# Input sums of two residues copied into PSUM ahead of the decay products, with the hand-written order of steps changed

## The chip, the cores and the metric

The kernel runs on one core of one Trainium2 chip. The time is the device time of one execution in microseconds; of several runs the median is given. A core has TensorE (PE, matrix products into PSUM), VectorE (DVE), ScalarE (ACT), GpSimd (POOL) and SyncE (SP, which here only issues DMAs). PSUM has eight banks, and a tile of 128 partitions by 512 f32 values fills one of them.

## The reference

For x of 2048 positions by 512 channels, two branches are mixed by a gate per position. Branch A is a diagonal complex state-space model with 512 states, branch B a linear attention with 32 heads of 16 and a softmax feature map. Cut to what matters here:

```python
# branch A: h_t = Lam_bar * h_{t-1} + (B_bar x_t),  y = 2 Re(C h) + D x
Bu = jnp.einsum("bld,pd->blp", x + 0j, B_bar)
for t in range(L):
    h = Lam_bar[None, :] * h + Bu[:, t, :]
# branch B: phi = concat(softmax(p), softmax(-p));  kv = sum phi_k v;  o = phi_q kv / phi_q z
o = num / den
# mix
out = g * a + (1 - g) * (o @ wo)
```

## The kernel before

Everything stays on the chip between the loads of the inputs and the stores of the output. The kernel is written as some 200 small generators, called steps (`st_...`), each of which issues a few instructions up to its next `yield`. The string `ORDER` is a list of 855 names. The loop at line 804 takes one name after the other and runs that generator one piece on. The four engines PE, DVE, ACT and SP execute their instructions in exactly this order, so the list is the schedule, written out by hand. Behind a name, `@5` gives the PSUM bank (or banks) that the piece takes, `:D` sends its copy or scaling to VectorE instead of ScalarE, `:A` an output's DMA to ScalarE's queue, and `F:28` puts 28 small idle matmuls (`spin`) on TensorE. The digit is the step's index; a name that comes twice runs its two pieces.

**Branch A.** The positions are dealt into eight residues r (position modulo 8), each with 256 positions. The states make four groups j of 128 states, each as two halves h of 64 states with real and imaginary parts.

- `l8` to `l15` load tiles of x transposed (tiles 0 to 7 are loaded ahead of the list). `NR` and `NI` load the two parts of B (`Bn`), `R0` to `R7` transpose it, `C..` and `J..` load C, `Q..` the query weights, `O` the output weights. All go through SyncE's queue. `c0` to `c7` scale C, two products and a sum each. `i0` to `i3` make the tables of sines and cosines.
- `g` r j (line 597) sums eight matmuls of x with B and, for odd r, products of the decay with the neighbours before. The result is the input sum that a block of positions up to r brings in. For r below 7 it is evicted to SBUF as `uv[j][:, r]` in bf16, for r = 7 to `va`.
- `z` j (line 622) runs the recurrence over the 256 blocks on VectorE and leaves the state at residue 7 in `H7`.
- `h` r j (line 660) makes the states of residue r: a power of the decay, as a diagonal block `dg`, times a state already there, plus `uv`. There are two ways to add `uv`. For the 20 pairs of `H_VECTOR` (r in 1, 2, 4, 5, 6) VectorE adds it while it evicts (line 672). For the other eight (r in 0, 3) TensorE multiplies `uv` by the identity (line 667) ahead of the decay's product (line 668), two matmuls of each per step, and ScalarE evicts (line 674). Residues 0, 1, 3 and 5 and their successors start from `H7`, so all `h` steps come behind their `z`.
- `y` n (line 711) multiplies the states of an output tile by C: two halves of four 512-column matmuls, and a tail of four 128-column ones with x and D. It accumulates in a PSUM bank that stays taken until `t` n.

**Branch B.** `W` and `f` fold the feature map into the key weights, `w` into the query weights. `k`, `v`, `q` n project tile n (four 512-column matmuls and an eviction). The features of keys (groups 0 to 4) and queries (groups A and 1 to 3) go through `x`/`X` (maximum tree and subtraction), `n`/`N` (the same with the minimum), `e`/`E` (exponentials on ScalarE, four tiles) and `s`/`S` (sums and normalisation on VectorE, with two small functions on ScalarE between). For queries `S` ends with four DMA transposes into `phT` (line 563). `a` n accumulates keys times values in two PSUM banks, which are given back by `Y` and `G` (the gate). `END` closes the first half's buffers; the query groups 1 to 3 come behind it.

`o` n (line 725) is the attention's numerator and denominator of tile n: two groups `pn` of four small matmuls from `phT`, evictions, a product on VectorE (`on`), and a transpose to `oT`, by DMA for n below 12 and on TensorE from 12 on. Tiles 0 to 3 use the features of group A, 4 to 7 those of group 1, 8 to 11 of group 2, 12 to 15 of group 3. `t` n (line 761) adds the output projection to y's bank, scales by the gate into `ot` and stores.

Of the kernel before, what the change touches and what calls it, by code (L numbers as in the profile page):

```python
# [29 lines left out]
k14 a0 n2 s1 k12 g20 x2 g00@6 k9 g30@0 s1 s1 s1 x2 n2 s1 v3 g40@4 x3 g01@3 g10@7 n3 R5 g00 a1 a1 x3 g60@1 n3 e2 R4  # L30
g11@6 g10 x3 g01 n3 e2 x3 e2 e2 n3 g11 k15@3 g60 g10 g30 g40 x3 s2 n3 g70@1 k15 g11 s2 x4 s2 s2 n4 g30 Q1 Q3 x4 n4 e3
e3 x4 C5 n4 Q0 x4 g50@7 g50 g50 s2 g21@4 n4 g21 s2 s2 v8@3 e3 e3 s3 g70 g70 g70 z0 s3 z0 g31@6 g31 s3 z0 z0 v11@0
g41@7 a2 C6 a2 g41 z0 z0 v11 g61@4 a2 g61 C7 w0@1 w0 C3 w1@7 w1 g31 a2 w2@0 w2 w3@4 s3 s3 g51@1 g51 g51 z0 R7 z0 x4
g62@7 w3 z0 z0 g71@6 g71 g02@0 v8 n4 s3 J2 g71 g71 z1 g02 z1 h50@1 h50 J2 z1 e4 e4 q1@4 h10@3 g62 g12@6 h10 g22@0 q2@1
z1 z1 z1 g22 q2 s3 z1 z1 q1 e4 h60@3 h60 g12 g12 z1 q3@7 q0@0 q0 q3 g32@1 e4 xA C2 g42@4 g32 nA g32 s4 g42 v9@6 v9 z1
s4 C0 J0 J0 g52@0 g52 c4 g52 nA c4 xA c4 R6 g72@7 g72 J1 s4 nA g23@3 g43@1 g03@4 g63@6 g72 g72 z2 h51@0 J3 c5 a3 g23
z2 J1 v10@7 h11@3 nA a3 c2 c2 g03 xA z2 z2 z2 z2 c0 h51 h61@4 z2 z2 g13@0 v10 xA h11 g43 c3 g13 a3 a3 J3 c5 z2 s4
g33@7 g13 g33 c0 z2 s4 s4 g33 h32@1 c2 h32 xA g53@3 g63 h52@0 g53 g53 nA s4 h52 h42@7 h42 eA c5 eA v14@1 v14 g73@6 g73
g73 q5@3 g73 h61 h12@0 h12 v12@1 v15@7 z3 z3 c0 z3 v12 eA eA h21@4 z3 v13@6 h21 a4 z3 z3 sA v13 z3 z3 c3 q10@0 q10
# [5 lines left out]
o2 y1 o2 t1 S1 S1 G G y9@5 y9 E2 E2 y4@2 y4 y2 N3 E2 E2 y5@6 y9 y5 t1 S1 S1 S1 S1 X3 t3 t3 y2 t2 t2 X3 N3 N3 S2 X3 S2
t0 o4@7 y5 o4 o4@4 o4 N3 o4 X3 S2 y4 t0 y13@0 S2 o4 o5@7 o5 o5@4 o5 o5 y6 o4 y6 o6@3 S2 o6 o6@7 o6 X3 o5 y7@4 y7 o5 S2
S2 o7@3 N3 y13 o6 t4 t0:A o6 o6 E3 E3 E3 S2 S2 y8@7 t4:D o7:D E3 S3 t5 S2 S2 S2 t5 y12@2 S3 S3 o7@3 o7 o7 o7 t6 t6
o8@6 o8 o8@3 o8 o7 y12 y8 S3 t1:A o8 o8 o9@1 o9 o9@6 o8 y11@3 y11 S3 S3 y10@1 o9 o9 o9 S3 S3 t4:A o11@6 y7 t7 y12 o9
o11 t7 o10@6 y8 t8 t8 y11 y13 o11@4 t9 S3 S3 S3 o10 o11 S3 o10@7 t9:D y15@6 y14@4 o11 o11 o10 o10 t8:A o12@7 o12 o12@5
# [19 lines left out]
def kernel(  # L69
# [44 lines left out]
    def bank(shape, dtype, name):  # L114
        return ps.tile(shape, dtype, tag=f"t{sel['banks'].pop(0)}", name=name, bufs=1)

    def evac(out_ap, in_ap):
        if sel["eng"] == "act":
            nc.scalar.copy(out=out_ap, in_=in_ap)  # L119
        else:  # L120
            nc.vector.tensor_copy(out=out_ap, in_=in_ap)
# [57 lines left out]
    G = const.tile([P, NTI], F32, name="G")  # L179
# [479 lines left out]

    def st_h(r, j):  # L660
        ph = bank([P, 2, NC], F32, "ph")
        add = (r, j) in H_VECTOR
        for h in range(2):
            t = 2 * j + h
            src = hs(r - 1, t, slice(0, NC)) if r in (2, 4, 6) else hs(7, t, slice(-1, NC - 1))
            if not add:
                MM(out=ph[:, h, :], lhsT=ident[:], rhs=uv[j][:, r, h, :], start=(h == 0), stop=False, skip_group_check=True)
            MM(out=ph[:, h, :], lhsT=dg[:, (r + 1) // 2 if r % 2 else 0, t, :], rhs=src, start=(add and h == 0), stop=True, skip_group_check=True)
# [179 lines left out]
```

## Time and profile before

| | us |
|---|---|
| median of 3 runs | 156.07 |
| lowest and highest | 155.94, 157.04 |
| the profiled execution, its own time | 156.63 |
| its span, first to last instruction | 154.6 |
| TensorE's weight loads, busy | 95.6 |
| GpSimd busy, all before 25 us | 16.1 |

The span leaves out about 2 us at the two ends. Busy time of an engine counts an instruction from its start to its end, and neighbours overlap by a part of their time. So the distance from one start to the next, which the timeline gives, is the better price of an instruction in a row of equal ones. TensorE's granted clock is 1.0 throughout.

This is how the busy shares go along the span, in 40 slices of 3.9 us:

```
PE   7999999999999999999999999999998999989990
DVE  3789999999999999999999999999997966423730
ACT  3489999999999999999999996799497998465652
DMA  4785998465475849910000006943169689789742
```

### The profile page before, as it was taken

Reading aid. Unit: us, or ns where it says so; the run is one execution under the profiler, and the core shown is the slowest. Engines: PE = TensorE matmul, PEld = TensorE weight load, DVE = VectorE, ACT = ScalarE, POOL = GpSimd, SP = SyncE. Lnnn points to the kernel's source line nnn. Section 1 sums busy time; section 2 is a strip of 40 time slices with the busy share of each in tenths; the row PEclk is TensorE's granted clock in tenths of the full one; section 3 lists DMA queues with packets and bytes.
Section 4 is the critical chain, followed back from the end, with each engine's and each line's share of the span. In section 5 each row is a group of like instructions: output and inputs, shape, how many; then the busy total and the mean of one; then the engine's idle time right before and its main releaser. Section 6 shows DMA issues by size and latency. Waiting matters only on the chain.

```text
span 154.6 us, 3382 instructions
## 1 busy us (share of the span) xinstructions
PE 147.7 (96%) x1254; PEld 95.6 (62%) x1254; DVE 131.8 (85%) x303; ACT 129.4 (84%) x279; POOL 16.1 (10%) x43
## 2 busy tenths in 40 slices
PE   7999999999999999999999999999998999989990
PEld 7844444797789876888755767454454545545540
DVE  3789999999999999999999999999997966423730
ACT  3489999999999999999999996799497998465652
POOL 8239980000000000000000000000000000000000
PEclk9999999999999999999999999999999999999999
DMA  4785998465475849910000006943169689789742
GB/s 120 158 222 87 168 191 170 89 98 107 97 78 105 174 94 168 184 25 6 0 0 4 0 0 136 141 136 68 34 123 143 117 163 197 150 137 200 208 147 94
DMA packets 50848, 17.55 MB, mean 113 GB/s; under 512 B 44176, under 2 KB 50832, under 8 KB 50832
## 3 DMA queue, kind: packets, MB, share of 16 engines
q1 hardware_dynamic: 48544, 15.36, 53.2%
q10 hardware_dynamic: 2128, 1.97, 4.5%
q8 instruction: 10, 0.16, 0.4%
q14 instruction: 6, 0.05, 0.1%
q0 software_dynamic: 160, 0.01, 0.1%
HBM read 2.64 MB, written 2.10 MB: 31 GB/s over the span
## 4 chain that ended last, share of the span: by engine, by line
DVE 47%; PE 32%; DMA 8%; ACT 6%; issue 4%; DVEq 0%; SPq 0%
PE py L717 9%; DVE smk L511 6%; PE pk L475 6%; DMA oT<-on 5%; PE py L765 5%; PE pgq L601 4%; DMA phT<-EEq 3%; DVE Bn L672 3%; DVE EEk L548 3%; DVE w L641 3%; DVE HM L672 3%; DVE H L652 3%; PE spin L812 3%; DVE EEk L527 2%; DVE EEk L521 2%
## 5 line engine op out<-in xcount | busy, mean ns | idle before, releaser
L601 PE MATMUL pgq<-xT,BT 128*128 128x256 bf16 x256 | 31.2, 272 | 0.0
L475 PEld LDWEIGHTS <-xT 128*128 128x128 bf16 x192 | 18.3, 98 | 18.6 <-DMA xT<-in_A_x_dram 0.8
L601 PEld LDWEIGHTS <-BT 128*128 128x128 bf16 x256 | 24.7, 98 | 3.9
L138 ACT ACTIVATE EEk<-EEk 128x1024 bf16<-128x1024 bf16 x20 | 20.6, 1075 | 0.3 <-DVE EEk L527 0.3
L765 PE MATMUL py<-Wo,oT 128*128 128x512 bf16 x64 | 16.1, 379 | 0.9 <-DMA oT<-on 0.9
L119 ACT CAST uv<-pgq 128x512 bf16<-128x512 f32 x28 | 16.3, 604 | 0.3
L475 PE MATMUL pq<-Wq,xT 128*128 128x512 bf16 x64 | 15.8, 379 | 0.0
L475 PE MATMUL pv<-Wv,xT 128*128 128x512 bf16 x64 | 15.6, 379 | 0.0
L475 PE MATMUL pk<-Wk,xT 128*128 128x512 bf16 x64 | 15.0, 379 | 0.3 <-ACT EEk L138 0.3
L138 ACT ACTIVATE ld<-pn 128x16 f32<-128x16 f32 x32 | 6.2, 193 | 7.6 <-PE pn L736 7.4
L138 ACT ACTIVATE EEq<-EEq 128x1024 bf16<-128x1024 bf16 x12 | 11.8, 1061 | 0.3 <-DVE EEq L527 0.3
L590 ACT ACTIVATE phT<-X,dgB 128x512 bf16<-128x512 bf16 x16 | 11.5, 740 | 0.0
L769 ACT ACTIVATE ot<-py,G 128x512 bf16<-128x512 f32 x12 | 8.0, 684 | 3.5 <-PE py L765 3.3
L119 ACT CAST nu<-pn 128x256 bf16<-128x256 f32 x28 | 10.3, 381 | 0.0
L736 PEld LDWEIGHTS <-phT 128*128 128x128 bf16 x128 | 6.7, 98 | 5.3 <-DMA phT<-EEq 1.2
L765 PEld LDWEIGHTS <-oT 128*128 128x128 bf16 x64 | 5.6, 97 | 6.2 <-DMA oT<-on 1.2
L119 ACT CAST vx<-pv 128x512 bf16<-128x512 f32 x16 | 9.4, 600 | 0.0
L548 DVE TENSOR_TENSOR EEk<-EEk,rck 128x4096 bf16<-128x4096 bf16 (+1 forms) x5 | 9.3, 1859 | 0.0
L119 ACT CAST Xq<-pq 128x512 bf16<-128x512 f32 x16 | 9.1, 610 | 0.2
L736 PE MATMUL pn<-KVm,phT 128*128 128x68 bf16 x128 | 8.0, 194 | 0.8 <-DMA phT<-EEq 0.7
L119 ACT CAST Xq<-pk 128x512 bf16<-128x512 f32 x15 | 8.4, 618 | 0.4 <-PE pk L475 0.4
L511 DVE TENSOR_TENSOR smk<-smk 128x512 bf16<-128x512 bf16 (+4 forms) x18 | 8.6, 476 | 0.1
(177 smaller groups left out, 319.6 us busy)
## 6 DMA issues: line engine op xcount, KB each, us to landing
X<-HM SPq DMA_DIRECT2D x8, 256.0 KB, 4.0
out_dram<-ot ACTq DMA_DIRECT2D x11, 128.0 KB, 2.5
out_dram<-ot SPq DMA_DIRECT2D x5, 128.0 KB, 2.5
C2r<-in_B_wqkv_dram ACTq DMA_DIRECT2D x2, 256.0 KB, 3.3
Wv<-in_B_wqkv_dram SPq DMA_DIRECT2D x1, 512.0 KB, 4.0
Bn<-in_A_B_re_dram SPq DMA_DIRECT2D x1, 512.0 KB, 5.5
Bn<-in_A_B_im_dram SPq DMA_DIRECT2D x1, 512.0 KB, 6.7
Wo<-in_B_wo_dram SPq DMA_DIRECT2D x1, 512.0 KB, 4.6
```

The lines of the kernel that those rows point to most:

```text
L119: nc.scalar.copy(out=out_ap, in_=in_ap)
L138: ins = nc.scalar.activation(**kw)
L475: MM(out=pt[:], lhsT=xT[:, kt, ti * P:(ti + 1) * P], rhs=W[:, kt, :], start=(kt == 0), stop=(kt == KT - 1))
L511: VT(out=dst, in0=cur[:, :, :, 0:n, :], in1=cur[:, :, :, n:2 * n, :], op=op)
L548: VT(out=E5, in0=E5, in1=rc.to_broadcast([P, L, 2 * NB, Dh, 4]), op=ALU.mult)
L590: nc.scalar.mul(out=t_, in_=x_, mul=c_)
L601: MM(out=pg[:, h, :], lhsT=BT[:, kt, 2 * j + h, :], rhs=xT[:, kt, r * NC:(r + 1) * NC], start=(h == 0 and kt == 0), stop=(r % 2 == 0 and k ...
L672: VT(out=dst, in0=ph[:], in1=uv[j][:, r], op=ALU.add)
L717: MM(out=py[:], lhsT=hs(r, t, slice(a * P, (a + 1) * P)), rhs=C2B[t], start=(t == 0), stop=False)
L736: MM(out=pn[:, 4 * m:4 * m + 4, :].rearrange("p h e -> p (h e)"), lhsT=ph[:, 4 * hf + m, :], rhs=KVm[:, 4 * hf + m, :], start=(m == 0), st ...
L765: MM(out=py[:], lhsT=oT[:, g, :], rhs=Wo[:, g, :], start=False, stop=(g == HG - 1))
L769: nc.scalar.mul(out=ot[:], in_=py[:], mul=G[:, ti:ti + 1])
```

## The change

In `st_h` the eight steps that used the identity matmuls get another first piece. The step takes its bank, copies `uv[j][:, r]` into it (bf16 in SBUF to f32 in PSUM, 128 x 512) and yields. Then the decay's two products are issued with `start=False`, so that they add to what stands in the bank. The eviction is as before. Each of these steps has three pieces now, and the list 863 names.

```diff
+H_SEED = tuple((r, j) for r in (0, 3,) for j in range(4))
...
     def st_h(r, j):
         ph = bank([P, 2, NC], F32, "ph")
         add = (r, j) in H_VECTOR
+        seed = (r, j) in H_SEED
+        if seed:
+            evac(ph[:], uv[j][:, r])
+            yield
         for h in range(2):
             t = 2 * j + h
             src = hs(r - 1, t, slice(0, NC)) if r in (2, 4, 6) else hs(7, t, slice(-1, NC - 1))
-            if not add:
+            if not add and not seed:
                 MM(out=ph[:, h, :], lhsT=ident[:], rhs=uv[j][:, r, h, :], start=(h == 0), stop=False, skip_group_check=True)
             MM(out=ph[:, h, :], lhsT=dg[:, (r + 1) // 2 if r % 2 else 0, t, :], rhs=src, start=(add and h == 0), stop=True, skip_group_check=True)
         yield
```

The list is new from end to end: the same steps, apart from the eight added pieces, in another order and with other banks. Its two beginnings, before and after, and its two stretches around `END`:

```diff
-B F:28 l11 F:4 W1@0 W0@1 W2@2 W1:D f1@3 W3@4 f1 W0:D f0@5 f0 NR W2:D f2@6 W3:D f3@0 f3 f2:D V@1 V P P P P2 P2 P2 P2 P2
+B NR l9 F:28 W1@0 NI W0@1 W2@2 W2 l10 W3@3 W1:D f1@4 W0:D f0@5 W3:D l14 f2@6 f0 f2 f3@0 f1:D V@1 V P f3:D U P P2 F:4
...
-h22@4 h31@2 h00@6 c6 q13@5 h31 h41@7 h43 c6 h22 h40@3 h63@2 h00 h41 h63 h40 h03@6 h03 sA sA y3@4 y3 END X1 o0@7 N1 X1
+h00@1 sA c7 sA q15@7 END o2@3 o2 X1 N1 h01 X1 N1 X1 o2@4 N1 X1 G o0@0 y0 q15 o2 y0 h01 N1 X1 N1 X2 o2 o2 h02 h02 X2
```

What moves, read from the two lists:

- Bn's two loads stand ahead of x's tiles 9 and 10; x's tiles come in the order 9, 10, 14, 13, 11, 8, 15, 12 instead of 11, 12, 10, 9, 14, 8, 13, 15 (both with other loads between). Of the 32 `spin` matmuls at the start four stand behind the folds now.
- Marks of the engine ahead of `END`: the eviction of `k6` and the copy of `W2` lose their D; the evictions of `f1` and `f3` have it and that of `f2` not; `i1` and `i2` have it for the absolute value where `i3` had it (`i0` in both); one product of `c5` has it. Behind `END` eleven pieces are marked in both lists: `o9`'s first eviction, two more of `o15`'s pieces, `t13` and `t15` gain the mark, one piece of `o12`, two of `o14`, `t9` and `t12` lose it.
- Around `END`: 15 of the 16 `q` evictions stand ahead of it instead of 12, and `y0`'s first half instead of pieces of `y6` and `y3`. The products and evictions of `h00`, `h01` and `h02` stand behind it, where only the eviction of `h01` did.
- The eight copies stand 2 to 54 names ahead of their products.

More of the change, by code (lines that the diff above doesn't have):

```diff
@@ L30 @@
[L30 to L39, printed above, removed]
@@ L45 @@
[L45 to L49, printed above, removed]
@@ L50 @@
-o12:D y15 o10 o12 o12 o11 o13@7 o13 o13@5 o13 o13 t2 y14 y14 o10 o12@7 t7:A t5:A o12:D o14@5 o14:D t3:A y10 o15@7 t9:A
-y10 o15 o15@5 o15:D o15 o13 t12 o15 o14@7 o14 o14 t12:D t12 t11 t11:D o15@5 o15 o13@7 t10 t6:A t11 y15 o13:D t10 t10
-t15 t15 t15:A o14 o14@2 t13 o14:D t13 t13 t14 t14 t14:A
-"""
-H_VECTOR = tuple((r, j) for r in (1, 2, 4, 5, 6) for j in range(4))
+B NR l9 F:28 W1@0 NI W0@1 W2@2 W2 l10 W3@3 W1:D f1@4 W0:D f0@5 W3:D l14 f2@6 f0 f2 f3@0 f1:D V@1 V P f3:D U P P2 F:4
+F:4 l13 k1@2 k1 P2 P2 P2 P2 P4 P4 P P3 V2@3 P4 l11 V2 k0@4 U i0 i0 i3 P2 P3 i3 i2 U i0 i0:D i2 k2@5 k0 x0 x0 n0 k3@1
@@ new lines @@
+R0 k3 v1@6 v0@7 x0 n0 k4@0 i3 i3 i0 i3 v1 i2 i2:D x0 k5@2 v5@3 n0 i1 k2 k7@4 n0 k6@1 i1 k5 x0 i1 i1:D x1 i1 k4 n0 R1
+l8 x1 k7 n1 n1 x1 l15 x1 n1 U v4@6 C7 x1 i2 n1 l12 k6 x2 R3 n1 L v3@5 e0 e0 k9@2 v7@0 v7 x2 v0 v6@4 v6 gw R2 v5 n2 n2
+v2@1 v2 s0 x2 s0 s0 R4 k14@0 s0 k13@7 s0 n2 M D k14 s0 e1 e1 s0 g00@4 g00 g10@3 k13 g20@1 g20 k11@0 k11 k9 g10 a0@47
+a0 s1 x2 s1 n2 s1 x2 g10 v3 k8@1 k8 s1 k15@0 n2 s1 s1 s1 k15 k10@2 k10 n3 v4 x3 g40@3 e2 k12@5 n3 x3 e2 n3 e2 k12 x3
+a1 a1 e2 g21@1 n3 g01@0 g01 g30@2 g70@6 g41@5 x3 g21 x3 n3 e3 g30 Q0 e3 s2 g40 g30 Q3 g11@0 x4 s2 s2 g11 g41 g61@1 s2
@@ new lines @@
+s2 g11 C0 s2 Q1 n4 x4 n4 g60@3 g60 C2 x4 e3 e3 g31@2 g50@5 n4 Q2 s2 v8@0 g50 g50 g61 g31 g31 R5 w2@3 C1 s3 a2 w2 a2
+w1@5 C4 w0@1 n4 w1 C6 g70 g70 a2 a2 s3 s3 x4 s3 w3@2 g70 x4 R6 z0 g51@3 z0 w0 w3 v11@5 s3 s3 n4 g22@6 v11 q2@1 g51 g22
+q2 g51 g02@2 v8 z0 z0 g62@5 z0 z0 z0 g02 z0 z0 z0 e4 g71@6 s3 g62 J1 g71 h50@1 g71 g71 z1 J0 z1 e4 C5 q0@3 h50 g12@0
+z1 z1 e4 z1 e4 q1@2 q1 q0 q3@5 q3 z1 s4 z1 C3 z1 g32@6 xA J0 nA g12 g12 J2 s4 z1 c4 v14@1 g42@2 g32 g42 nA h60@3 g32
+z1 xA h60 v14 g52@5 g52 g52 xA a3 c2 h10@0 J1 s4 h32@2 J2 c2 c2 R7 g63@6 J3 J3 h51@1 h51 h10 c3 g72@5 g72 g72 g03@3
@@ new lines @@
+g72 c5 g23@1 nA v9@0 s4 c3 v9 z2 z2 c5:D v10@5 g03 v10 g43@0 a3 a3 z2 z2 g23 z2 z2 a3 nA c6 s4 s4 c4 g43 z2 z2 g13@3
+g13 g13 xA z2 z2 h12@5 h32 g33@1 h32 g33 h52@0 xA nA h12 q6@3 c3 c4 g63 h31@2 g33 g53@6 g53 h31 q6 s4 eA h52 g53 eA
+g73@5 g73 g73 g73 h11@1 eA eA c5 h11 h42@3 v13@6 O h42 v12@0 v12 z3 z3 h62@1 h62 z3 v13 z3 z3 v15@5 v15 c0 sA z3 sA
+h30@3 z3 c0 sA q4@1 q4 q11@0 q11 z3 h31 sA sA h33@6 a4 a4 q7@5 a4 a4 Y Y z3 q5@1 c6 q5 sA sA h61@0 z3 q7 h61 q9@2 h33
+q14@4 c0 c1 h33 h30 h13@1 sA sA Y h21@0 h21 h13 q9 c1 c1 q14 sA c7 q10@5 q10 h53@6 h53 G q8@2 q8 h43@0 q13@4 h43 c6
@@ new lines @@
+h63@1 h63 q13 h23@6 h23 y0@5 h41@2 c7 h20@0 h41 q12@4 h03@1 h30 h03 h01@6 h03 h20 h40@3 h02@2 Y h40 q12 h22@0 h22
+h00@1 sA c7 sA q15@7 END o2@3 o2 X1 N1 h01 X1 N1 X1 o2@4 N1 X1 G o0@0 y0 q15 o2 y0 h01 N1 X1 N1 X2 o2 o2 h02 h02 X2
+o1@3 o0 o0@7 h00 o1 o1@4 y4@6 o1 o1 N2 X2 N2 X2 o2 o0 o0 y2@2 y5@0 y2 y2 o0 E1 E1 E1 E1 y1@3 y1 y12@4 o3@7 o3 o1 y12
+y12 X2 o3@7 o0 S1 G S1 S1 N2 h00 t2 t0 o3 o3 S1 S1 G o1 N2 o3 o3 S1 t2 t2 y9@1 S1 N2 S1 y1 y3@7 X3 t0 N3 y5 y5 E2 E2
+E2 t1 E2 X3 X3 X3 N3 t1 X3 S2 y3 y6@2 y3 t3 y13@5 t3 N3 S1 o4@3 o4 o4@7 o4 o4 y6 S2 S1 o5@3 o5 o4 S1 S1 S2 o4 S2 o5@7
@@ new lines @@
+o5 o5 y9 y9 t1:A S2 o6@3 o6 o6@7 o6 o6 y13 y13 N3 o5 o5 N3 S2 S2 o6 o6 E3 S2 y4 y4 t4 t4:D E3 y8@3 E3 y6 E3 S2 S2 t5
+S2 S2 o7@7 o7:D o7@6 o7 o7 o7 S3 t6 y8 y8 S3 y10@7 t6 t5 t4:A S3 t5:A o8@6 o8 o8@2 o8 o7 S3 y11@0 o8 o8 o9@6 o8 S3 S3
+o9:D o9@2 o9 o9 y11 o9 o9 S3 y10 o10@2 o10 S3 y7@6 t6:A o11@2 o11 y7 y7 o10@2 o10 o10 o10 t7 t7 t8 t8 t9 y10 S3 S3 S3
+o11@2 t9 o11 y15@6 o11 o11 S3 o11 o12@3 o12 o12@1 o10 y14@2 t7 y11 o12 o12 o12 t9:A o13@3 o13 o13@1 o13 y14 o12@3
+o14@1 t0:A y15 o14 o14@1 o14 o14 t3:A o12:D t12 o15@3 o15:D o15@1 o15:D o15 o14 t11 t10 o15 o13 o13 o15@3 t12 t12:A
@@ L55 @@
+o15:D o14@1 t8 o13@4 o13:D y14 t10 t10:A o14 t11:D t11:A y15 t15 t15:D t15 t13 t13:D t14 t14 t13 t14:A
+"""
+H_VECTOR = tuple((r, j) for r in (1, 2, 4, 5, 6,) for j in range(4))
+H_SEED = tuple((r, j) for r in (0, 3,) for j in range(4))
 OT_PE = (12, 13, 14, 15)
```

8 lines of the change are left out of this document (removed).

## The prediction

> **What bounds the kernel now.** I read the page's busy times first, then sums over stretches, then the chain of waits, then single rows of the timeline for prices.
>
> ```profile
> PE 147.7 (96%) x1254; PEld 95.6 (62%) x1254; DVE 131.8 (85%) x303; ACT 129.4 (84%) x279; POOL 16.1 (10%) x43
> ```
>
> ```profile
> 28.00:97.00 69.00, 69.00 (x688) 53.24 (x687) 68.55 (x141) 66.26 (x123) 0.00 (x0) 1.00 0.41 76
> 97.00:113.00 16.00, 15.88 (x111) 7.96 (x110) 15.92 (x33) 12.81 (x35) 0.00 (x0) 1.00 0.45 90
> ...
> 118.00:151.00 33.00, 32.12 (x272) 17.71 (x272) 18.41 (x35) 22.90 (x73) 0.00 (x0) 1.00 0.83 169
> ```
>
> The columns of such a stretch are its length, then busy time of TensorE, its weight loads, VectorE and ScalarE. From 28 to 97 us three engines are full at once: TensorE for all 69.00, VectorE for 68.55, ScalarE for 66.26. After 118 only TensorE is. So removed matmuls are worth something only where TensorE itself is what everybody waits for. The chain shows where that is:
>
> ```profile
> 35.77 1.23 DVE EEk L521
> ...
> 111.77 1.24 DVE EEq L559
> 113.06 4.83 DMA phT<-EEq
> 117.94 0.30 PE pn L736 x4
> ...
> 151.04 0.69 ACT ot L769
> ```
>
> From 35.77 to 113.06 the chain is VectorE's, nearly without break. Then it is the transfer that turns query group 1 (phT), and from 117.94 (the first step of o4) TensorE. So VectorE's list and ScalarE's exponentials set the start of o4, and what TensorE has left behind it sets the end. I price the change by these two.
>
> **Prices.** In the timeline a row is start, time, engine, line and operation, with the count of neighbours put together; the distance of starts is what an instruction costs its engine:
>
> ```profile
> 88.36 0.27 PE L667 MATMUL ph<-uv,ident 128*128 128x256 bf16 x1
> 88.47 0.27 PE L668 MATMUL ph<-H,dg 128*128 128x256 bf16 x1
> ...
> 26.32 3.06 ACT L119 CAST Xq<-pk 128x512 bf16<-128x512 f32 x6
> 29.19 0.69 ACT L119 CAST uv<-pgq 128x512 bf16<-128x512 f32 x1
> ...
> 84.69 1.36 ACT L590 ACTIVATE phT<-X,dgB 128x512 bf16<-128x512 bf16 x2
> 85.93 1.08 ACT L119 CAST Xq<-pq 128x512 bf16<-128x512 f32 x2
> ```
>
> A 256-column matmul takes 0.11 us of TensorE. The change drops 8 steps x 2 = 16 of them: -1.75 us.
>
> Eight seeds come in, a 128x512 copy from SBUF into PSUM each. The words of the change allow either engine, but no seed in the list carries the mark D, so all are ScalarE's. The trace has no ScalarE write to PSUM. Nearest rows: an eviction costs (29.19 - 26.32)/6 = 0.48, a scaled copy that reads SBUF (85.93 - 84.69)/2 = 0.62. The second has a scale per partition, which the seed has not, and the next rows tell what that costs:
>
> ```profile
> L590 ACT ACTIVATE phT<-X,dgB 128x512 bf16<-128x512 bf16 x16 | 11.5, 740 | 0.0
> L769 ACT ACTIVATE ot<-py,G 128x512 bf16<-128x512 f32 x12 | 8.0, 684 | 3.5 <-PE py L765 3.3
> L119 ACT CAST uv<-pgq 128x512 bf16<-128x512 f32 x28 | 16.3, 604 | 0.3
> L121 DVE CAST Xq<-pk 128x512 bf16<-128x512 f32 x1 | 0.7, 678 | 0.0
> L121 DVE COPY Xq<-ptw 128x512 bf16<-128x512 bf16 x4 | 1.5, 420 | 0.6 <-PE ptw L274 0.6
> L455 DVE TENSOR_SCALAR kk<-psi 128x256 uint32<-128x256 uint32 x2 | 0.6, 282 | 0.0
> ```
>
> 684 - 604 = 80 ns is the scale, so a seed is 0.62 - 0.08, about 0.53, bounds 0.48 and 0.62. Sum: +4.2 us (3.8 to 5.0). [...]
>
> Steps that change engine ahead of END: k6's eviction and W2's copy go to ScalarE (+0.48 each); one more fold eviction (-0.48), one more absolute value in i (-0.31) and one product of c5 (-0.62) go to VectorE. ScalarE -0.46. VectorE by the durations above: -0.68 - 0.42 + 0.68 + 0.28 + about 0.35 = +0.2; c5's product is the estimate, between 0.28 and 0.42.
>
> **VectorE, up to o4.** It does the same features in the same order, 0.2 dearer, and G's last two small steps (about 0.25 together) now stand ahead of S1's final product. It has 0.5 us of idle in the 85 us from 28 to 113 to give back. In the first ten microseconds it has more, and there four of the 32 opening matmuls are moved behind the folds:
>
> ```profile
> 1.11 3.59 PE spin L812 x32
> ...
> 7.22 7.13 SPq L229 DMA_TRANSPOSE xT<-in_A_x_dram  x5
> 14.40 0.74 SPq L284 DMA_DIRECT2D Bn<-in_A_B_re_dram  x1
> ```
>
> ```profile
> 7.63 3.45 PE pk L475 x16
> ```
>
> ```profile
> xT<-in_A_x_dram SPq DMA_TRANSPOSE x16, 4.1
> ```
>
> That brings the weights' transposes forward by at most 4 x 0.11 = 0.45. Against it, both loads of Bn pass tiles of x on SyncE's queue. Tile 9 leaves after the first Bn load, near 13.7 (7.22 + 4 x 1.43 + 0.74), and lands 4.1 later, the median of these transfers, at 17.8 or somewhat after. k9 has 13 tiles of 0.86 us ahead of it and, from a first tile at 7.6 as now, is due on TensorE near 18.8. So 0 to 0.5 of stall, hidden as long as TensorE has spare time at o4 (below). I let the two cancel. By VectorE the landing for o4 goes from 117.94 to about 118.3.
>
> **ScalarE, up to o4.** VectorE's sum of S1 reads the exponentials of E1:
>
> ```profile
> 102.98 3.94 ACT L138 ACTIVATE EEq<-EEq 128x1024 bf16<-128x1024 bf16 x4
> 106.96 1.23 DVE L511 TENSOR_TENSOR smq<-EEq 128x2048 bf16<-128x2048 bf16 x1
> ...
> 28.00:103.00 75.00, 74.88 (x740) 56.27 (x739) 74.55 (x153) 71.30 (x142) 0.00 (x0) 1.00 0.44 84
> ```
>
> E1 ends at 106.92, the sum starts at 106.96: no slack. In the new list ScalarE has 4.65 us more to do up to there: 4.2 - 0.46 = 3.8, two evictions' worth (three of q moved ahead, two of h0 moved behind, net +0.5) and 0.35 of small steps. From 28 to 103 it idles 75.00 - 71.30 = 3.7 us. That is the low bound of what is free: after a gap an instruction also loses the 0.12 (604 ns against a distance of 0.48) by which neighbours overlap, and a dozen gaps would make it about 5.2, an estimate. So need and room are about equal. I take E1 0.5 late, between 0 and 2. o4 then starts at 118.8.
>
> **TensorE, from o4 on.** Counted in the two lists and priced by these rows:
>
> ```profile
> 118.25 0.22 PE py L722 x4
> ...
> 119.68 0.26 PE pn L736 x8
> 119.94 0.86 PE py L717 x4
> ```
>
> From o4 to o12: 16 groups of pn (0.13), 14 halves of y (0.86), 8 tails of y (0.22) and 6 t (0.86), 21.1 us. After: 16, 13, 7 and 6, 20.0. From o12 to the end the counts are equal (8 pn, 3 halves, 3 tails, 6 t, 4 transposes). So 1.1 of the 1.75 us is saved behind o4 and 0.65 ahead of it; the latter only makes TensorE wait longer for phT. It runs dry at 117.2 now:
>
> ```profile
> 115.32 1.89 PE L765 MATMUL py<-Wo,oT 128*128 128x512 bf16 x8
> 117.94 0.30 PE L736 MATMUL pn<-KVm,phT 128*128 128x68 bf16 x4 [0.73 <-DMA phT<-EEq]
> ...
> 134.30 6.69 SPq L563 DMA_TRANSPOSE phT<-EEq  x4
> 137.07 1.04 PE L765 MATMUL py<-Wo,oT 128*128 128x512 bf16 x4 [0.57 <-DMA oT<-on]
> 142.68 0.30 PE L736 MATMUL pn<-KVm,phT 128*128 128x68 bf16 x4
> ...
> DMA to landing us min/median/max: 2.8/3.7/4.8
> ```
>
> It would be dry at 116.5 then, with 2.3 us of spare time up to 118.8: this cover takes 0.5 of stall at k9, or late evictions, without cost. From o4 (117.94) to o14 (142.68) it takes 24.74 now. After: 118.8 + 24.74 - 1.1 = 142.4 with the oT wait of 0.57 kept, 141.9 without. But o14 also needs the third transfer of group 3. These leave from 134.30, 1.67 apart, so the third leaves near 137.7 and with up to 4.8 lands by 142.5: o14 is on time to within 0.2 us now. S3's steps stand behind the numerators of o8 and o9, which follow o4, so this landing shifts with o4 rather than with the saving: 142.4 to 143.5. I take o14 at 142.5, -0.2, and the same 12 us to the end. The profiled run's own time is 156.63 for a span of 154.6, the median of the three runs 156.07. **Forecast: 155.9** (own range 154.9 to 157.0).
>
> **Rivals.** (1) ScalarE becomes the bound. Of some 5.2 us of gaps all but 0.55 must vanish for E1 to be on time. Against: the gaps come from waits that a new order can remove, and half of their 3.7 us are two waits that stand around END:
>
> ```profile
> ACT Wk L119 <- PE ph L668: 1.1, 1, 1.1
> ACT ld L138 <- PE pn L736: 0.8, 1, 0.8
> ```
> For: the seed adds a wait of TensorE on ScalarE, with TensorE's whole queue behind it, and its bank is held from the seed to the eviction. If 3 us of the gaps stay, E1 is 2.5 late, o4 at 120.8, o14 at 144.4 to 145: +2.0, 158.1. It decides from about 1 us of lateness on. (2) VectorE's path shortens: the opening's 0.45 comes through, ScalarE is on time and S3 is placed earlier against the waits it has after 113 (18.41 busy of 33). Then the whole removal counts: 156.07 - 1.75 = 154.3. For it speaks that TensorE is the 96% engine, against it that the chain up to 113 is not TensorE's. (3) The third transfer holds o14 fully: o4's 0.4 to 0.9 late is passed on and nothing is saved, 156.7. (4) The change doesn't do what it says: seeds on VectorE would leave ScalarE free and cost VectorE 8 x 0.42 to 0.68 by its two copies above; there is no mark D, so I give it nothing.
>
> **How the numbers follow.** Forecast 0.36, rival 1 0.34, rival 2 0.15, rival 3 0.15. One per cent of 156.07 (154.5 to 157.6) is about what this kernel's measurement tells from no change. Rival 2 lies below, with little of the forecast: faster 0.16. Rival 1 lies above but for its mild end: slower 0.32. The rest, 0.52, is within. For eight in ten I go down to rival 2's 154.3 and up past rival 1's 158.1 to 158.5, where most of its 3 to 5 us of gaps stay.
>
> **What would show it.** 16 rows fewer of the identity matmul and 8 ScalarE copies of about 0.65 us into ph confirm the edit. E1 ending before 107.5 and o4 starting between 118 and 119 confirm the middle; o4 after 120 with VectorE waiting for ScalarE's exponentials is rival 1; o4 before 117.5 is rival 2. At the end, a wait for phT ahead of o14 shows rival 3. I am wrong in kind if TensorE shows new idle in 28 to 97 that VectorE shares, or if k9 or the first g steps wait for transfers for over a microsecond.

## The result and the profile after

The changed kernel takes 157.15 us (median of 16 runs, 155.77 to 158.47), the kernel before 156.41 beside it (16 runs, 155.77 to 157.04). The ratio is 1.0042, interval [1.0023, 1.0060]: slower by about 0.7 us, where 0.2 less was forecast. The profiled executions say the same: spans of 155.42 and 154.62. Ratios, here and below, leave out slow runs (at a lower granted clock, or more than 1.5% above the fastest of their kernel), so they are not the quotients of the medians, and start times in such a run are not compared.

The page's busy line of the changed kernel, then the stretches that were shown of before (columns: length, busy time of TensorE, weight loads, VectorE, ScalarE):

```profile
PE 147.0 (95%) x1238; PEld 93.2 (60%) x1238; DVE 132.6 (85%) x304; ACT 132.9 (85%) x286; POOL 14.5 (9%) x43
```

```profile
28.00:97.00 69.00, 68.06 (x652) 49.57 (x651) 67.95 (x138) 68.07 (x129) 0.00 (x0) 1.00 0.43 83
...
97.00:113.00 16.00, 15.96 (x118) 8.69 (x117) 15.97 (x37) 14.37 (x40) 0.00 (x0) 1.00 0.41 57
118.00:151.00 33.00, 31.50 (x268) 17.24 (x267) 19.77 (x39) 23.27 (x74) 0.00 (x0) 1.00 0.86 165
```

Between 28 and 97 us TensorE is no longer busy for all 69.00 us but for 68.06, VectorE has lost 0.60, and ScalarE, with the copies, is nearly full (66.26 before). The copies are there, eight of them, all on ScalarE, and TensorE has 16 matmuls fewer (1238 for 1254). Two rows of the timeline give a copy's price:

```profile
76.49 0.62 ACT L120 CAST ph<-uv 128x512 f32<-128x512 bf16 x1
77.01 0.62 ACT L120 CAST uv<-pgq 128x512 bf16<-128x512 f32 x1
```

Where the time went is seen at two landmarks of VectorE's row, the first scan (z0) and the first step of query group 1's maximum tree (X1). Before, from the timeline:

```profile
48.52 1.27 DVE L641 TENSOR_TENSOR_SCAN w<-ssm_par,ut 128x256 bf16<-128x256 f32 x2
...
97.92 0.69 DVE L511 TENSOR_TENSOR mxq<-Xq 128x1024 bf16<-128x1024 bf16 x1
```

And after, with the start of the fifth attention tile (o4):

```profile
52.15 1.27 DVE L642 TENSOR_TENSOR_SCAN w<-ssm_par,ut 128x256 bf16<-128x256 f32 x2
...
99.64 0.69 DVE L512 TENSOR_TENSOR mxq<-Xq 128x1024 bf16<-128x1024 bf16 x1
...
118.88 0.42 PE L741 MATMUL pn<-KVm,phT 128*128 128x68 bf16 x8
```

X1 starts 1.72 us later (99.64 against 97.92). From X1 to the end of the span it is 55.78 us instead of 56.70, so 0.92 us shorter. 1.72 - 0.92 = 0.80 is the difference of the spans. Most of the 0.92, namely 0.78, lies between X1 and o4 (19.24 us instead of 20.02); behind o4 only 0.14 is left. The scan itself can't be compared between the lists, because the new one places more VectorE work ahead of it.

These are single executions. Two later kernels have the same code up to X1 as one of these two: there X1 is at 98.37 (old list) and 99.95 (new list). So the new list's X1 is 1.3 to 2.0 us late, and a difference of a few tenths at X1 means little.

Up to X1 VectorE is busy 93.49 of 97.92 us before and 94.16 of 99.64 after. So 1.05 of the 1.72 us is idle time, and 0.67 is busy time. The idle part builds up before 50 us. The same columns as above, before and then after:

```profile
0.00:28.00 28.00, 26.43 (x162) 14.69 (x163) 24.02 (x85) 22.48 (x44) 16.06 (x43) 1.00 0.78 156
28.00:50.00 22.00, 22.00 (x269) 18.89 (x268) 21.97 (x43) 21.53 (x39) 0.00 (x0) 1.00 0.55 97
50.00:97.00 47.00, 47.00 (x422) 34.36 (x420) 46.58 (x99) 44.73 (x84) 0.00 (x0) 1.00 0.34 66
```

```profile
0.00:28.00 28.00, 25.98 (x174) 15.22 (x175) 23.57 (x85) 21.61 (x42) 14.47 (x43) 1.00 0.83 157
28.00:50.00 22.00, 21.35 (x251) 17.07 (x250) 21.47 (x39) 21.53 (x41) 0.00 (x0) 1.00 0.59 100
...
50.00:97.00 47.00, 46.71 (x402) 32.49 (x401) 46.48 (x101) 46.55 (x89) 0.00 (x0) 1.00 0.35 75
```

Ahead of 50 us VectorE is busy 0.95 us less than before (0.45 and 0.50), TensorE 1.10 less. From 50 to 97 VectorE is as full as it was. Two rows of the changed kernel's timeline name the largest pieces of this idle time behind 28 us. TensorE's:

```profile
35.03 1.16 PE L602 MATMUL pgq<-xT,BT 128*128 128x256 bf16 x9 [0.65 <-DMA BT<-Bn]
```

And VectorE's:

```profile
48.80 1.22 DVE L522 TENSOR_TENSOR EEk<-Xq,mxk 128x2048 bf16<-128x2048 bf16 x1 [0.32 <-PE kvacc L579]
```

TensorE waits for a transposed tile of B that has not landed. VectorE waits 14 us later for TensorE to have done with one of the two feature buffers (`EEk`).

At the other end of the stretch TensorE was expected to wait for the transfer of query group 1, as it had for 0.73 us. It doesn't. These rows, ahead of o4, follow each other without a break, and the transfer (issued at 114.89) landed 3.26 us later, at 118.15:

```profile
114.89 5.37 SPq L564 DMA_TRANSPOSE phT<-EEq  x4
```

```profile
117.16 1.03 PE L770 MATMUL py<-Wo,oT 128*128 128x512 bf16 x4
118.02 1.03 PE L722 MATMUL py<-C2r,Bn 128*128 128x512 bf16 x4
```

So o4 starts 0.73 us after its features are there, when TensorE comes to it. In every trace below with the new list around o4 it starts 0.2 us or more behind the landing; with the old list and no copies it is 0.05.

### The profile page after: what moved, and what is told of

It reads as the page before. It is cut to its first block, busy times and chain, and to the rows that moved or that the text cites. A ratio compares the mean times of both kernels' runs of the same rounds, so it can differ in the third digit from the quotient of the medians.

```text
span 155.4 us, 3357 instructions
## 1 busy us (share of the span) xinstructions
PE 147.0 (95%) x1238; PEld 93.2 (60%) x1238; DVE 132.6 (85%) x304; ACT 132.9 (85%) x286; POOL 14.5 (9%) x43
## 4 chain that ended last, share of the span: by engine, by line
PE 33%; ACT 20%; DMA 16%; SPq 14%; DVE 13%; issue 2%; ACTq 0%
PE pgq L602 12%; SPq L230 10%; DMA oT<-on 7%; PE pq L476 5%; PE py L770 4%; DMA Bn<-in_A_B_im_dram 4%; PE py L722 3%; ACT Xq L120 3%; ACT phT L591 3%; DMA BT<-Bn 3%; DVE smq L512 3%; SPq L289 2%; ACT EEk L139 2%; DVE EEq L522 2%; ACT uv L120 2%
## 5 line engine op out<-in xcount | busy, mean ns | idle before, releaser
L770 PE MATMUL py<-Wo,oT 128*128 128x512 bf16 x64 | 15.6, 380 | 1.5 <-DMA oT<-on 1.4
L749 DVE TENSOR_TENSOR on<-nu,rd 128x512 bf16<-128x512 bf16 x16 | 6.5, 421 | 7.6 <-ACT rd L139 7.4
L591 ACT ACTIVATE phT<-X,dgB 128x512 bf16<-128x512 bf16 x15 | 11.0, 749 | 0.0
L120 ACT CAST nu<-pn 128x256 bf16<-128x256 f32 x28 | 10.8, 411 | 0.0
L120 ACT CAST Xq<-pk 128x512 bf16<-128x512 f32 x16 | 9.1, 606 | 1.0 <-PE pk L476 1.0
L512 DVE TENSOR_TENSOR smk<-smk 128x512 bf16<-128x512 bf16 (+4 forms) x18 | 8.1, 448 | 0.2
```

The lines of the kernel that those rows point to most:

```text
L512: VT(out=dst, in0=cur[:, :, :, 0:n, :], in1=cur[:, :, :, n:2 * n, :], op=op)
L591: nc.scalar.mul(out=t_, in_=x_, mul=c_)
L749: VT(out=on[:].rearrange("p g h (a b) -> p (g h) a b", b=4), in0=nu[:].rearrange("p c h (a b) -> p (c h) a b", b=4), in1=rd[:].unsqueeze(2 ...
L770: MM(out=py[:], lhsT=oT[:, g, :], rhs=Wo[:, g, :], start=False, stop=(g == HG - 1))
```

## The experiments

All ratios are against the kernel before, run beside each experiment on the same chip. The changed kernel's 1.0042 is the mark.

**Copies against identity, in both lists.** The first experiment keeps the new list and puts the identity products in the place of the copy:

```diff
         if seed:
-            evac(ph[:], uv[j][:, r])
+            for h in range(2):
+                MM(out=ph[:, h, :], lhsT=ident[:], rhs=uv[j][:, r, h, :], start=(h == 0), stop=False, skip_group_check=True)
             yield
```

> The new list as it is, but the first piece of the eight steps issues the two identity matmuls instead of the ScalarE copy: 1.75 us more on TensorE, 4.2 us less on ScalarE. Theory A (ScalarE is the bound from 72 to 102 us, and the freed matmul time comes back as waits for evictions): the two about cancel, within 0.5 us of the changed kernel (ratio to before 1.002 to 1.008), ScalarE no longer full. Theory B (the new list itself is slower, at its start and at its end, while the copies do save their matmuls): about 1.2 us slower than the changed kernel, ratio to before 1.010 to 1.014.

158.26 us, ratio 1.0113 [1.0089, 1.0136], as theory B had it. With the identity the new list is 1.1% slower than the old one; the copies bring 0.7% of it back, about 1.1 us. The trace places only a part of that: from z0 to X1 it is 48.07 us here and 47.49 with the copies, so 0.58 us.

The second leaves the input sums of residues 0 and 3 out altogether, neither copied nor multiplied:

```diff
         if seed:
-            evac(ph[:], uv[j][:, r])
+            pass
             yield
...
-            MM(..., start=(add and h == 0), stop=True, ...)
+            MM(..., start=((add or seed) and h == 0), stop=True, ...)
```

> The new list without any input sum for residues 0 and 3 (neither copy nor identity matmul, so those states lack it): TensorE as in the changed kernel, ScalarE 4.2 us less. Theory A: TensorE gets back the 1.4 us that it loses between 70 and 103 us, o4 starts near 117.5 instead of 118.9, ratio to before 0.993 to 0.998. Theory B: no change against the changed kernel, ratio 1.003 to 1.006.

157.39 us, 1.0064 [1.0040, 1.0088], no faster than with the copies. ScalarE is lighter by eight copies (66.16 us busy from 28 to 97 instead of 68.07) and X1 still starts at 99.50. In the new list the copies cost nothing that can be measured. Beside this run the identity products cost 0.5%, about 0.8 us, so 0.8 to 1.1 us is what the copies are worth.

The third puts seven copies into before's list, each where its bank comes free:

```diff
+H_SEED = tuple((r, j) for r in (0, 3) for j in range(4) if (r, j) != (3, 3))
...
+        seed = (r, j) in H_SEED
+        if seed:
+            evac(ph[:], uv[j][:, r])
+            yield
...
-            if not add:
+            if not add and not seed:
```

> The list of before with seven of the eight copies, each put where its bank comes free (4 to 17 names ahead of the product); h33 keeps its identity matmuls. TensorE 1.5 us less, ScalarE 3.7 us more. Theory A: ScalarE falls behind between 70 and 103 us, E1 ends 1 to 2 us later than 106.9, ratio to before 1.003 to 1.012. Theory B: the copies alone are a gain, ratio 0.990 to 0.997.

158.9 us, 1.0167 [1.0140, 1.0194], the largest loss of the three and beyond theory A's range. Its waits between 80 and 100 us (who waits, for whom, us in total, times, longest) say why:

```profile
DVE C2i L596 <- ACT phT L592: 1.4, 1, 1.4
DVE dlk L555 <- ACT lgk L140: 1.0, 1, 1.0
```

ScalarE does the same work later, and VectorE waits 2.4 us for it; before's kernel shows no such waits there. X1 starts at 100.09, 2.17 later than before. TensorE waits for ScalarE too (1.3 us ahead of one decay product), and each copy holds its bank for longer; this run doesn't tell these two apart. So ScalarE as the bound is real, but in the old list. The new list has made room for the copies.

**The order of the early transfers.** Two kernels change only SyncE's order. In one the load of C for `C7` goes behind three transposes of B:

```diff
-... l15 x1 n1 U v4@6 C7 x1 i2 n1 l12 k6 x2 R3 n1 ... R2 ... R4
+... l15 x1 n1 U v4@6 x1 i2 n1 l12 k6 x2 R3 n1 ... R2 ... R4 C7
```

> The changed kernel with one transposed load of C (C7, not needed before 60 us) moved on SyncE's queue from ahead of tile 12 and the transposes R3, R2, R4 to behind them, so that these leave 1.3 us earlier. The wait of 0.8 us at 34 us for R2's landing goes. Theory A: TensorE, 0.8 us earlier from 35 us on, is stopped by ScalarE later on: no change, ratio to before 1.002 to 1.006. Theory B: 0.5 to 0.8 us faster than the changed kernel, ratio 0.998 to 1.001.

156.74 us, 1.0011 [0.9985, 1.0036]. The wait at 35 us went, waits of 0.85 us for a tile of x ahead of 23.19 and of 0.47 for B ahead of 26.00 came, and X1 was at 99.65.

In the other the tiles come in the order of use, and two transposes of B ahead of `C7`:

```diff
-NR l9 NI l10 l14 l13 l11 R0 R1 l8 l15 C7 l12 R3 R2 R4
+NR l9 NI l14 l13 l11 l8 R0 R1 l15 l10 l12 R2 R3 C7 R4
```

> The changed kernel with only the order of SyncE's early transfers altered: x's tiles 10 and 12 and the two transposes of B that group 1 needs ahead of C7's, the tiles in the order in which the key steps use them (9, 14, 13, 11, 8, 15, 10, 12). Theory F (the time is lost because the new list's front lets TensorE wait for transfers, 1.0 us more by 35 us than before, and VectorE gets that passed on through its two feature buffers): the wait of 0.79 us at 34.2 us goes, no other of over 0.4 us comes, VectorE's subtraction ahead of END starts 0.5 to 0.9 us earlier than 99.6, and the time falls by 0.5 to 0.9 us against the changed kernel, to a ratio of 0.998 to 1.001. Theory R (what is late is VectorE's own order of work behind 35 us, and the front's waits are covered): less than 0.3 us of gain, ratio 1.003 to 1.005.

156.98 us, 1.0015 [0.9992, 1.0039], X1 at 99.04, a wait of 0.2 us for B. X1 fits theory F; the ratio lies between the ranges of F and R. Both intervals overlap the changed kernel's, and a later kernel with the same code up to X1 (below) had X1 at 99.95. This alone doesn't settle it.

**Joining the two lists.** Before's first 140 or 220 names with the changed rest, and the reverse:

> The first 140 names of before's list (to about 22 us), the other names in the changed kernel's order, with the eight ScalarE copies; three pieces get another PSUM bank. Theory F: half or more of the 1.0 us goes, since both early loads of B and the tiles are issued as before: ratio 0.997 to 1.001. Theory R: as the changed kernel, 1.003 to 1.005.

> The first 220 names of before's list (to about 35 us), the others in the changed kernel's order, with the eight copies; 37 pieces get another bank. Theory F: the whole front's loss goes, TensorE stands at 35 us where it stood before the change, the feature subtraction ahead of END (99.6) comes 0.8 to 1.3 us earlier, and with the copies' gain of 1.1 us kept the kernel is faster than before: ratio 0.992 to 0.998. Theory R: nothing changes behind 50 us, ratio 1.002 to 1.005.

> The reverse: the first 220 names of the changed list, the others in before's order, with the identity products and no copies; 23 pieces get another bank. Theory F: slower than before by the front's 0.6 to 1.2 us, ratio 1.004 to 1.008. Theory R: as before, 0.998 to 1.002.

1.0305 [1.0281, 1.0329], 1.0302 [1.0255, 1.0348] and 1.0448 [1.0416, 1.0479], far above every expected range. All three engines have gaps behind the seam (in the first, TensorE is busy 5.71, VectorE 4.44 and ScalarE 4.84 of the 8 us from 28 to 36). The likely reason is that each half was written to fit the other, and its neighbour and banks are gone. These runs say nothing on the theories. One thing can be read: X1 is 3.75 us later than in the changed kernel in the first of them (103.39), and the span is 3.84 longer (159.26). In this pair the lateness at X1 goes through to the end.

**Taking work from one engine.** First VectorE, ahead of the first scan:

```diff
-            VT(out=E5, in0=E5, in1=rc.to_broadcast([P, L, 2 * NB, Dh, 4]), op=ALU.mult)
+            if p != 1:
+                VT(out=E5, in0=E5, in1=rc.to_broadcast([P, L, 2 * NB, Dh, 4]), op=ALU.mult)
```

> The changed kernel without the scaling of key group 1's features by their reciprocal sums (one VectorE product of 1.22 us at about 28 us; those features stay unnormalised). Theory V (VectorE's chain up to the subtraction and maximum tree of group 1, which started at 99.64, sets the end; the removed time is worth its full length): the tree starts at 98.4 to 98.7 and the time falls by 0.8 to 1.1 us against the changed kernel, ratio to before 0.996 to 0.999. Theory T (TensorE is late by itself in the front, and VectorE would only wait longer for it through the two feature buffers): the tree at 99.3 or later, gain under 0.3 us, ratio 1.002 to 1.005.

157.93 us, 1.0066 [1.0039, 1.0094], no gain, as in theory T, though above its range. From its timeline:

```profile
48.99 1.22 DVE L522 TENSOR_TENSOR EEk<-Xq,mxk 128x2048 bf16<-128x2048 bf16 x1 [0.41 <-PE kvacc L580]
...
52.34 0.68 DVE L643 TENSOR_TENSOR_SCAN w<-ssm_par,ut 128x256 bf16<-128x256 f32 x1
...
99.86 0.68 DVE L512 TENSOR_TENSOR mxq<-Xq 128x1024 bf16<-128x1024 bf16 x1
```

1.22 us less to do, and the subtraction, the scan and X1 are each 0.2 us later. VectorE's own work is not what sets the first 50 us. Behind the scan VectorE is full: from z0 to X1 it takes 47.52 us here, 47.49 in the changed kernel and 47.41 without any input sums. It isn't alone in that stretch, as the 48.07 with the identity products show.

Then TensorE, between X1 and o4:

```diff
         for kt in range(KT):
             xs = xT[:, kt, ti * P:(ti + 1) * P]
-            MM(out=py[:, kt * P:(kt + 1) * P], lhsT=xs, rhs=Dd[:, kt, :], start=False, stop=False)
+            if n not in (0, 1, 2, 3, 5, 12):
+                MM(out=py[:, kt * P:(kt + 1) * P], lhsT=xs, rhs=Dd[:, kt, :], start=False, stop=False)
```

> The changed kernel without the 24 small products of D and x of the six output tiles that come ahead of the fifth attention tile (1.3 us of TensorE between 99 and 118 us; those tiles lack that term). Theory V: TensorE is full there only because it is ahead of a transfer that lands at 118.15; the fifth tile starts 0 to 0.7 us earlier than 118.88 and the time falls by 0 to 0.5 us. Theory T: TensorE alone sets the end, the time falls by 0.9 to 1.3 us, ratio 0.996 to 0.999.

157.11 us, 1.0017 [0.9989, 1.0045]: some 0.4 us of gain for 1.3 us of work, in theory V's range, though the intervals overlap. So TensorE holds o4, but only by the 0.7 us that it is behind the transfer; with that gone the transfer is next.

**Moving work from VectorE to ScalarE.** Two steps of residue 5 leave `H_VECTOR`, in the new list with the other transfers and in the old one. ScalarE then evicts them, and TensorE adds their sums by the identity:

```diff
+H_VECTOR = tuple(p for p in H_VECTOR if p not in ((5, 0), (5, 1)))
```

> The kernel with the altered order of early transfers (ratio 1.0015), and the steps of residue 5 of groups 0 and 1 taken from VectorE's adding to the identity products with ScalarE's eviction: VectorE loses 2 x 0.60 us ahead of 99 us, TensorE gets 2 x 0.22, ScalarE 2 x 0.48. Theory V: the tree of group 1 starts at 97.9 to 98.2 instead of 99.04, the time falls by 0.5 to 1.0 us, ratio 0.995 to 0.998. Theory T, or ScalarE full: no gain, ratio 1.000 to 1.004.

> Before's kernel, list and all, with the same two steps moved from VectorE's adding to the identity and ScalarE. Theory V: the tree of group 1 starts at 96.7 to 97.0 instead of 97.92; TensorE waited 0.73 us for the transfer of the fifth attention tile, so of the 1.2 us 0.5 to 0.9 reach the end: ratio 0.994 to 0.997. Theory S (in the old list ScalarE has no room, as the copies showed there): VectorE gets the waits for ScalarE instead, the tree starts no earlier than 97.9, ratio 1.000 to 1.006.

1.0086 [1.0052, 1.0120] and 1.0035 [1.0014, 1.0055], both slower than what they were made from, the first by more than any theory allowed. X1 is at 99.83 in the new list and 98.53 in the old. VectorE's waits from 28 to 75 us in the new one:

```profile
DVE smk L514 <- ACT EEk L141: 1.0, 1, 1.0
DVE mc L631 <- ACT va L122: 0.6, 1, 0.6
```

ScalarE has no room for two more evictions there (it is busy 46.58 of the 47.00 us from 50 to 97). VectorE waits longer for exponentials and evictions than the 1.2 us it was spared.

**The waits behind o4.** In the changed kernel TensorE waits for transposed attention tiles (`oT`) ahead of t8 and t4:

```profile
135.66 1.02 PE L770 MATMUL py<-Wo,oT 128*128 128x512 bf16 x4
137.83 1.90 PE L770 MATMUL py<-Wo,oT 128*128 128x512 bf16 x8 [1.15 <-DMA oT<-on]
```

```diff
-t4 t4:D E3 y8@3 E3 y6
+y8@3 t4 t4:D E3 E3 y6
...
-t7 t7 t8 t8 t9 y10 S3 S3 S3 o11@2 t9 o11 y15@6 o11 o11 S3
+t7 t7 y10 o11@2 o11 y15@6 t8 t8 t9 S3 S3 S3 t9 o11 o11 S3
```

> The changed kernel with two places of the list behind the fifth attention tile altered, nothing else: ahead of t8, for whose transposed tile TensorE waited 1.15 us at 136.7, stand y10's tail, o11's second products and y15's first half (1.2 us of work), and ahead of t4, waited for 0.30 us at 123.9, stands y8's first half. Theory W (the 1.1 us that TensorE saves behind the fifth tile are lost in these waits): 0.7 to 1.2 us of gain against the changed kernel, ratio to before 0.996 to 1.000. Theory X (those waits only take up time that a transfer behind them, phT of group 3 which landed at 142.59, would take anyway): the fifteenth tile starts no earlier than 143.0, gain under 0.3 us, ratio 1.002 to 1.006.

> The same two places altered in the kernel with the other order of early transfers (ratio 1.0015 there). If both causes hold and add: 1.0 to 1.7 us of gain against the changed kernel, ratio 0.993 to 0.998, faster than before. If only the early one holds: 0.999 to 1.003.

1.0050 [1.0021, 1.0080] and 1.0051 [1.0021, 1.0080]; the second missed both its ranges. The waits for t4 and t8 are gone and others stand in their place, in the first kernel:

```profile
137.32 1.02 PE L723 MATMUL py<-C2r,Bn 128*128 128x512 bf16 x4 [0.43 <-ACT ot L775]
...
140.84 0.29 PE L742 MATMUL pn<-KVm,phT 128*128 128x68 bf16 x4 [0.58 <-ACT ot L775]
```

The earlier products find their PSUM banks still held, until ScalarE has scaled the tiles in them. From o4 to the fifteenth tile it is 24.20 us in both, 0.39 less than before the edit; but o4 came 0.32 later in both traces, and the times show no gain. Theory X had the outcome right, with another holder: a bank, not the transfer of group 3. The second kernel has the transfers in order of use, and X1 at 99.95.

The same in before's list, where t9 had waited 0.57 us:

```diff
-o11@4 t9 S3 S3 S3 o10 o11 S3 o10@7 t9:D y15@6
+o11@4 S3 S3 S3 o10 o11 S3 o10@7 y15@6 t9 t9:D
```

> Before's kernel with one place altered: the output product t9, for which TensorE waited 0.57 us at 137, stands behind o10's and o11's next pieces and y15's first half (1.0 us of work). Theory W: gain of 0.3 to 0.7 us, ratio 0.995 to 0.998. Theory X (phT of group 3, landed at 142.63 for the fifteenth tile at 142.68, holds it): ratio 0.999 to 1.002.

1.0003 [0.9975, 1.0031]: no gain.

**Which engine holds the front.** VectorE's product left out again, now with the transfers in order of use:

> The kernel with the other order of early transfers, without the scaling of key group 1's features (a VectorE product of 1.22 us at about 28 us, those features stay unnormalised); in the changed kernel that brought nothing (group 1's tree at 99.86 instead of 99.64). Theory P (transfers held TensorE, and TensorE held VectorE, in the first 50 us; with the transfers mended VectorE's own chain is next): the tree starts 0.5 to 1.1 us earlier than 99.04. Theory Q (TensorE or ScalarE holds VectorE there whatever the transfers do): it starts within 0.3 us of 99.04, and the time is that of the kernel with the product, ratio 0.999 to 1.004.

1.0021 [0.9994, 1.0047], X1 at 99.67. The time is theory Q's, VectorE is held there whatever the order of transfers; X1 is 0.63 later than 99.04, outside Q's window too, and inside the spread of 99.04 to 99.95. Then TensorE, alone and with VectorE:

```diff
         for h in range(2):
-            for kt in range(KT):
+            kts = KT // 2 if (r, j) in ((0, 1), (3, 0), (4, 1), (6, 0), (6, 1)) else KT
+            for kt in range(kts):
...
```

> The changed kernel without half of the products of x and B in five of branch A's input sums (20 matmuls x 0.11 = 2.2 us of TensorE between 36 and 43 us; those sums lack half of their terms). Theory T (in the new list's first 50 us TensorE, full, is what VectorE waits for: through the two feature buffers and the sums that the first scan needs; 1.2 us less VectorE work in that stretch brought nothing): the first scan starts 0.6 to 1.2 us earlier than 52.15, group 1's maximum tree earlier than 99.64 by as much, and the time falls by 0.5 to 1.2 us against the changed kernel, ratio 0.997 to 1.001. Theory V (VectorE's own order of work sets the first scan): the scan starts at 51.9 or later and the time is the changed kernel's, ratio 1.002 to 1.006.

156.79 us, 0.9990 [0.9960, 1.0020]: 0.5% below the changed kernel, and the intervals just part. That is theory T's range for the time. In the second, the value products of tiles 0, 3, 4 and 5 are halved in the same way, and the VectorE product of the earlier run is left out:

> The same, and besides half of the products of four value tiles (8 matmuls x 0.22 = 1.7 us of TensorE before 21 us) and the scaling of key group 1's features (1.22 us of VectorE at 28 us) left out: both engines are lighter ahead of the first scan. Theory T: VectorE's own stalls and work come into play only once TensorE is lighter, so that now the 1.2 us of VectorE count too: first scan 1.5 to 2.6 us earlier than 52.15, group 1's tree as much, and the time 1.0 to 2.0 us below the changed kernel's, ratio 0.991 to 0.998, unless the end is held by what comes behind the tree. Theory D (the transfers of x's tiles and of B hold the front, whatever the engines have to do): no more than 0.5 us, ratio 1.000 to 1.005.

156.38 us, 1.0002 [0.9978, 1.0027], theory D's range, and no faster than the one before it. X1 starts at 98.66, 0.98 us earlier, less than theory T asked for and more than theory D, for 3.9 us less of TensorE and 1.2 less of VectorE. TensorE's rows show where the rest went:

```profile
18.63 1.04 PE L477 MATMUL pk<-Wk,xT 128*128 128x512 bf16 x4 [1.21 <-DMA xT<-in_A_x_dram]
23.05 1.90 PE L477 MATMUL pk<-Wk,xT 128*128 128x512 bf16 x8 [0.80 <-DMA xT<-in_A_x_dram]
35.36 3.23 PE L605 MATMUL pgq<-xT,BT 128*128 128x256 bf16 x28 [0.98 <-DMA BT<-Bn]
```

As soon as TensorE is lighter it stands 3.0 us waiting for tiles of x and of B. The reading that fits these runs is that in the new list's first 50 us TensorE and the transfers hold together, and VectorE follows. Two profiles with the changed order of work agree: the first key product starts at 8.05 in the changed kernel and at 7.14 in the one with `C7` moved, and X1 at 99.64 and 99.65. An earlier start only became longer waits for tiles.

## Why the prediction was wrong

**The prices were right.** A copy's successor starts 0.52 us after it (76.49 to 77.01), where 0.53 was estimated; behind each of the eight copies it is 0.51 to 0.52. The copies' durations are longer (587 to 720 ns, mean 659), because each overlaps with its successor. ScalarE's room was also right: with the copies it is busy 68.07 of 69.00 us, and not over.

**The step that failed, in the sum,** is the one behind o4: "118.8 + 24.74 - 1.1". The 1.1 us were not saved. From o4 to o14 it took 24.59 us (118.88 to 143.47) after 24.74, so 0.15 less. o14 had been taken at 142.5, and the 0.97 that it came later is nearly all that the span was off (155.42 for 154.4). These are the two stretches, before and after:

```profile
117.94:142.68 24.74, 24.16 (x209) 13.50 (x209) 14.13 (x25) 18.37 (x61) 0.00 (x0) 1.00 0.89 163
```

```profile
118.88:143.47 24.59, 23.14 (x202) 12.58 (x201) 14.15 (x27) 18.36 (x61) 0.00 (x0) 1.00 0.94 165
```

The matmuls did go: TensorE is busy 1.02 us less. Its idle time in the stretch rose from 0.58 to 1.45 us and took the gain. The prediction left the one wait for `oT` as it was (0.57) or dropped it; in its place came 1.15 and 0.30. Other traces with the same order behind o4 did no better: 24.87 to 26.18 in the two experiments on the input sums in this list, the two on the transfers, and the one that lightens VectorE. With the two waits gone, in the experiments on them, TensorE waited for banks instead and 24.20 was left. Rival 3, a hold of o14 by its transfer, didn't happen: that landed at 142.59 and o14 started at 143.47. "The same 12 us to the end" is right (11.95 after 11.94).

**The step that failed ahead of o4** is "So 0 to 0.5 of stall, hidden as long as TensorE has spare time at o4 (below). I let the two cancel", with the 2.3 us of that spare time. There was none: TensorE was to run dry at 116.5 and was busy up to 118.88. And the two did not cancel. X1 came 1.72 us late, and S1's final product 1.88 late (113.65 against 111.77). Of the 1.72 the part that is busy time, 0.67, had been put at 0.2. VectorE had been read as having 0.5 us of idle time from 28 to 113, so nothing behind the scan could take a delay up: 47.5 us of work stand there in one piece. The prediction had its own warning, "TensorE shows new idle in 28 to 97 that VectorE shares", and this is what the rows at 35.03 and 48.80 are. How the front's lateness reaches VectorE is shown only in part: less VectorE work ahead of the scan changed nothing, so VectorE waited for others there, and the one wait that the trace names is the 0.32 us for a feature buffer.

**E1** was expected 0.5 us late because of ScalarE. It ended at 108.54, 1.61 late, about as late as X1; without 4.2 us of copies it ended at 108.33. Rival 1 has its mechanism in the old list only. Rival 2 fell with X1, and rival 4 falls because the copies are all ScalarE's.

**o4 at 118.8** came true (118.88) by luck, by errors that cancel. VectorE's final product of S1 came 1.88 late and not 0.4 to 0.9, but the first transfer of group 1 landed after 3.26 us instead of 4.83, and then o4 waited for TensorE. With a transfer as long as before's it would have landed near 119.7 (114.89 + 4.83, an estimate).

**What stays open.** Which names of the new front make it late was not found. The order of SyncE's transfers gave 0.3% at most (some 0.5 us) and no clear verdict, and parts of the two lists could not be exchanged. Why the first transfer of group 1 is shorter in the new list is open too; a second trace of each list repeats it (3.19 and 4.95). No kernel tried was clearly faster than before.

## What to carry to other kernels

Where several engines are full in turn, ask for every stall which engine gets it next, and look for slack there; spare time that the old order had a hundred microseconds later is no cover until it is found again in the new one. Matmuls taken out of a stretch shorten it only if the transfers and banks behind them come earlier too; here 1.02 us of work went and 0.87 came back as idle time. Count a changed order as a change of its own: here the edit gained about 1 us and the order that made room for it lost more. And a hand-made order is a fit of the whole list: removing one wait in it, or joining two good halves, mostly brings the next wait forward.

## What was not expected of the hardware

In the changed kernel's trace a 512-column step of VectorE overlaps with the next instruction, in most pairs by 0.08 us; where that one reads its result, it starts 0.03 us after the step's end. From the timeline:

```profile
17.76 0.41 DVE L512 TENSOR_TENSOR mnk<-Xq 128x512 bf16<-128x512 bf16 x1
18.21 0.29 DVE L512 TENSOR_TENSOR mnk<-mnk 128x256 bf16<-128x256 bf16 x1
```

And further on, from the same view:

```profile
42.57 0.42 DVE L512 TENSOR_TENSOR mnk<-mnk 128x512 bf16<-128x512 bf16 x1
42.90 0.28 DVE L512 TENSOR_TENSOR mxk<-mxk 128x256 bf16<-128x256 bf16 x1
```

In the first pair the second instruction reads what the first has written; the second pair changes from one tree to the other. The same 512-column step costs 0.45 us ahead of its own reader and 0.33 ahead of another tree's step. Eight such bf16 steps in the whole trace stand right ahead of their reader, and all eight cost 0.45 or 0.46; nearly all the others cost 0.33 or 0.34. So such a step right ahead of its own reader costs 0.12 more in this trace. Counted in the two timelines, VectorE has 21 pairs of neighbours ahead of X1, of all widths, where the second starts 0.03 to 0.04 us after the end of the first, whose result it reads, and the old list has 13. At 0.12 each that is about 1 us, an estimate from the 512-column steps, most of it ahead of the first scan; no run here takes it out, so what it costs the kernel is not shown. And transfers of one kind differ much: the first transposes of groups 1 to 3 took 3.26, 3.26 and 3.77 us to land in the changed kernel, where before's first took 4.83.
